# A two-batch double step for the last two hidden slices, closer attention visits, and new places for sums of weights, in a fused attention and SwiGLU kernel

## Chip, core and metric

The kernel runs on one core of a Trainium2 chip. Its metric is the device time of one execution in microseconds. The engines are named as the profile names them: PE is TensorE (matmuls), DVE is VectorE, ACT is ScalarE, POOL is GpSimd, and SP is SyncE, which here only issues DMAs. Each engine works through its own list of instructions in the order of the program, and waits at an instruction until what it needs is there.

## The reference

Sigmoid attention over 8 batches, 12 heads, 448 positions and head width 64, followed by a gated feed-forward block over the 3584 rows that the attention gives:

```python
scores = scale * np.matmul(q, k.transpose(0, 1, 3, 2)) - np.log(S)
attn = 1.0 / (1.0 + np.exp(-scores))
attn_out = np.matmul(attn, v)                 # (8, 12, 448, 64)
x = attn_out.transpose(0, 2, 1, 3).reshape(3584, 768)
g = x @ w_gate                                # (768, 1536)
val = x @ w_val
out = (g * sigmoid(g) * val) @ w_out          # (1536, 768)
```

All inputs and the output are float32.

## The kernel before

**Attention.** The work is cut into 24 units, numbered n = 0 to 23; unit n is four heads of batch n // 3. Its q and k are loaded by SP into four staging slots (`stg_a`, two per unit), cast to 16 bits (`casts`, L843, on POOL from unit 4 on), and transposed by two DMAs on SP's queue (`trans`, L847). Each unit has seven tiles of scores, (n,0) to (n,6): four small matmuls (`qk_tile`, L246), then a sigmoid on ACT (`sig_tile`, L263) into `pt_a`. When all seven are there, 28 small matmuls with v (`pv`, L276) give the rows of x, which DVE copies out of PSUM.

**Feed-forward.** Batches go in pairs, pb = 0 to 3. The hidden width is cut into 12 slices of 128. For pairs 0 and 1 the first half (FFN1) is done slice by slice and batch by batch: `ffn1(b, f)` (L331) has 12 matmuls of 448 columns. Pair 2 did slices 0 to 9, and pair 3 all slices, by *double steps*: `double(pb, (f, f+1))` (L434) takes two slices for both batches of the pair in seven products (a Strassen-Winograd scheme), 7 x 3 x 2 = 42 matmuls, where four `ffn1` units have 48. The scheme needs sums of x (`x_sums`, L411, four kinds for each of three j) and sums of the weights (`fast_w`, L376, kinds 3, 1, 2, 4 for each group of three slices). Kind 4 of x is used in the sixth of the seven products, kind 3 in the fifth.

The second half (FFN2) is always done in the same scheme: `ffn2_group` (L595) is a generator whose seven steps are products of six matmuls of 384 columns, in two PSUM banks in turn; DVE (or ACT) reads each product out before the next but one may write the bank. Groups 0, 1 and 2 take the columns 0 to 383 of each pair's rows, group 3 of pair 1 the rest of pairs 0 and 1. For that rest, `rest_sums` (L584) makes 24 small sums on POOL, in storage that group 0 has used. Sums of the hidden rows are made by `make_sums` (L533) on DVE.

**The order.** A list `units` of FFN work with planned times is merged with the attention *visits* (L955 to L968): a visit makes the score tiles of half a unit, either (n,0) to (n,3) with `pv(n-1)` in its middle, or (n,4) to (n,6). When visit (n,4) to (n,6) has been written into the program, the plan of L951 follows it: POOL waits for the last sigmoid of unit n (`behind_visit`, L864), casts unit n+2, SP transposes it, POOL issues the loads of its v, and SP issues the loads of unit n+4. Below, "visit (n,0)" is the one of four tiles and "visit (n,4)" the one of three.

PSUM is a ring of four tiles of two banks (L72). A group of FFN2 keeps its tile from the first to the last of its seven products (`kept`, L598), and visits go round the rest; when no group is open, a visit of four tiles places its last two so that one of them falls on the fourth tile (L790).

In the second half of pair 1 the products and the visits alternate by the planned list: visit (19,4), four products, visit (20,0), three, (20,4), four, (21,0), three, (21,4), four, (22,0). The other three visits, (22,4), (23,0) and (23,4), stand between the four `ffn1` units of slices 10 and 11. `rest_sums` stands in the first product of `part((1,), ...)` (L753), ahead of visit (19,4). After the last product of group 3 come the sums of x for pair 2, on POOL (L759).

## Time and profile before

| | |
|---|---|
| median of 3 runs | 399.17 us (399.03 to 399.38) |
| the profiled execution, time and span | 399.09 us, 397.1 us |
| PE busy | 386.6 us (97%), 3110 matmuls |
| DVE busy | 251.2 us (63%) |
| ACT busy | 237.4 us (60%) |
| POOL busy | 124.6 us (31%) |
| granted PE clock, mean | 0.999 |
| second half of pair 1 begins | 206.15 us |
| double steps of pair 2 begin, end | 257.32, 297.06 us |

The span runs from the first to the last instruction of the profiled execution; the time of that execution is 2.0 us longer. A line of the timeline gives the start of a run of equal instructions in us from the span's start, its length, engine, line of the kernel, operation, what is written and read, and how many there are; in square brackets stands the time for which the engine had been idle, and who ended it. [...] the pitch of matmuls is read from the starts. The chain of waits is followed back from the last instruction to whatever released it.

### The profile page before, as it was taken

What the parts mean: (1) busy time and instruction counts of PE and PEld (TensorE: products, weight loads), DVE (VectorE), ACT (ScalarE), POOL (GpSimd) and SP (SyncE); (2) the same over time, 40 slices, a digit from 0 to 9 for tenths busy, and PEclk for the clock granted to TensorE, in tenths of its full rate; (3) what the DMA queues carried; (4) which work ended last, traced back from release to release, by engine and by line L of the source; (5) the groups of instructions that cost most, each with busy time, mean ns of one, the idle gap of its engine ahead of it and who ended that gap; (6) DMA issues with size and microseconds to landing.
All of it is one profiled execution on the core that took longest, in us unless ns stands there. A gap on an engine that the chain in (4) does not pass through costs nothing.

```text
span 397.1 us, 8117 instructions
## 1 busy us (share of the span) xinstructions
PE 386.6 (97%) x3110; PEld 201.3 (51%) x3110; DVE 251.2 (63%) x504; ACT 237.4 (60%) x385; POOL 124.6 (31%) x204
## 2 busy tenths in 40 slices
PE   6799999999999999999999999999999999999995
PEld 2444545445555444444455554455556655555663
DVE  2737656688643454466675564799986568787553
ACT  5965885746467787779772567866653066656000
POOL 3638141432311352333337539600007400000900
PEclk9999999999999999999999999999999999999999
DMA  8999989998599777797778699000000520000055
GB/s 254 261 246 256 245 168 215 197 190 118 150 275 241 165 166 161 163 186 164 167 162 199 113 208 238 2 2 1 2 0 2 158 79 2 2 2 0 2 172 146
DMA packets 65590, 54.39 MB, mean 137 GB/s; under 512 B 36048, under 2 KB 61744, under 8 KB 65552
## 3 DMA queue, kind: packets, MB, share of 16 engines
q1 hardware_dynamic: 49264, 36.97, 37.3%
q0 software_dynamic: 15376, 15.34, 24.6%
q10 hardware_dynamic: 912, 1.57, 1.2%
q8 instruction: 24, 0.39, 0.4%
q14 instruction: 14, 0.11, 0.1%
HBM read 47.19 MB, written 11.01 MB: 147 GB/s over the span
## 4 chain that ended last, share of the span: by engine, by line
PE 89%; DMA 4%; DVE 2%; issue 1%; SPq 1%; ACT 1%; POOL 1%; DVEq 0%; POOLq 0%; ACTq 0%
PE ps_D L324 27%; PE ps_D L633 24%; PE ps_D L460 22%; PE ps_D L254 8%; PE ps_D L289 7%; DMA ramp_a<-in_k_dram 2%; DMA stg_a<-in_k_dram 1%; DMA T<-c 1%; PE ps_D L223 1%; POOL c L204 1%; SPq L211 1%; DVE xT L312 0%; DVE T L229 0%; ACT pt_a L273 0%; SPq L166 0%
## 5 line engine op out<-in xcount | busy, mean ns | idle before, releaser
L273 ACT ACTIVATE pt_a<-ps_D 128x896 f16<-128x896 f32 x148 | 127.2, 921 | 40.9 <-PE ps_D L254 39.4
L324 PE MATMUL ps_D<-xT,wg 128*128 128x448 f16 x312 | 69.0, 354 | 0.2
L324 PE MATMUL ps_D<-xT,wv 128*128 128x448 f16 x312 | 68.5, 353 | 0.0
L349 DVE TENSOR_TENSOR t<-ps_D,s 128x448 f16<-128x448 f32 x52 | 32.4, 624 | 54.5 <-ACT s L347 54.0
L470 ACT ACTIVATE snap<-ps_D 128x448 f32<-128x448 f32 x66 | 34.3, 541 | 29.0 <-PE ps_D L460 28.4
L254 PE MATMUL ps_D<-T,T 64*64 64x448 bf16 x644 | 44.1, 357 | 1.6 <-DVE T L229 1.0
L324 PEld LDWEIGHTS <-wg 128*128 128x128 f16 x312 | 27.8, 98 | 33.7 <-issue 11.7
L324 PEld LDWEIGHTS <-wv 128*128 128x128 f16 x312 | 30.4, 98 | 28.6 <-issue 0.4
L347 ACT ACTIVATE s<-ps_D 128x448 f16<-128x448 f32 x52 | 28.7, 552 | 22.6 <-PE ps_D L324 22.6
L633 PEld LDWEIGHTS <-S 128*128 128x128 f16 x312 | 30.2, 98 | 21.1 <-issue 1.4
L633 PE MATMUL ps_D<-ramp_a,S 128*128 128x384 f16 x234 | 40.5, 327 | 0.0
L204 POOL CAST c<-stg_a 128x896 bf16<-128x896 f32 x40 | 36.4, 936 | 12.0 <-DMA stg_a<-in_q_dram 10.7
L289 PE MATMUL ps_D<-pt_a,v 64*64 64x448 f16 x672 | 35.9, 350 | 0.0
L353 DVE SCALAR_TENSOR_TENSOR hT<-ps_D,t 128x448 f16<-128x448 f32 x52 | 32.5, 625 | 5.4
L651 DVE SCALAR_TENSOR_TENSOR osb<-ps_D,osb 128x384 f32<-128x384 f32 x40 | 22.3, 557 | 18.7 <-PE ps_D L633 14.0
L862 POOL CAST held<-S 128x1 bf16<-128x1 f16 x3 | 0.6, 188 | 105.4 <-ACT osb L644 55.7
L646 DVE TENSOR_SCALAR osb<-ps_D 128x384 f32<-128x384 f32 x37 | 20.6, 557 | 19.2 <-PE ps_D L633 16.2
L633 PEld LDWEIGHTS <-hT 128*128 128x128 f16 x228 | 22.1, 98 | 15.6 <-issue 1.2
L460 PE MATMUL ps_D<-xS,wv 128*128 128x448 f16 x132 | 28.6, 353 | 0.0
L862 POOL CAST held<-pt_a 128x1 bf16<-128x1 f16 x13 | 2.5, 189 | 82.0 <-ACT pt_a L273 82.0
L254 PEld LDWEIGHTS <-T 64*64 64x64 bf16 x644 | 15.4, 105 | 24.0 <-issue 16.6
L460 PE MATMUL ps_D<-xT,wg 128*128 128x448 f16 x132 | 26.8, 353 | 0.0
(109 smaller groups left out, 497.7 us busy)
## 6 DMA issues: line engine op xcount, KB each, us to landing
out_dram<-osb SPq DMA_DIRECT2D x45, 192.0 KB, 3.7
stg_a<-in_q_dram SPq DMA_DIRECT2D x18, 448.0 KB, 5.6
stg_a<-in_k_dram SPq DMA_DIRECT2D x18, 448.0 KB, 6.5
v<-in_v_dram POOLq DMA_DIRECT2D x38, 112.0 KB, 4.5
wg<-in_moe_w_gate_dram POOLq DMA_DIRECT2D x4, 576.0 KB, 11.6
wv<-in_moe_w_val_dram POOLq DMA_DIRECT2D x4, 576.0 KB, 12.4
wo<-in_moe_w_out_dram POOLq DMA_DIRECT2D x4, 576.0 KB, 8.4
stg_a<-in_q_dram POOLq DMA_DIRECT2D x3, 448.0 KB, 13.8
```

Source lines behind the costliest of these rows:

```text
L204: eng.tensor_copy(out=t.rearrange("p c h d -> p h c d"), in_=st.rearrange("p h (c d) -> p h c d", c=C))
L254: nc.tensor.matmul(out=sc[g:g + 64, h2, :S], lhsT=kt[r, w * 64:(w + 1) * 64], rhs=qt[r, :, w * 64:(w + 1) * 64], start=True, stop=True,)
L273: nc.scalar.activation(out=pt, in_=sc[:, :, :S], func=SIGM, bias=sbias, scale=qkscale)
L289: nc.tensor.matmul(out=P[g:g + 64, h2, :S], lhsT=vt[r, h2, c * D:(c + 1) * D], rhs=pt[r, h2, :], start=(c == 0), stop=(c == C - 1),)
L324: nc.tensor.matmul(out=D.t[:, i, :S], lhsT=(wg16, wv16)[i][f // FW][:, pr, cs], rhs=xT[(b, pr)], start=(pr == 0), stop=(pr == NP - 1),),
L347: D.read(nc.scalar.activation(out=s16, in_=D.t[:, 0, :S], func=SIGM), 0)
L349: D.read(nc.vector.tensor_tensor(out=t1, in0=D.t[:, 0, :S], in1=s16, op=MULT), 0)
L353: nc.vector.scalar_tensor_tensor(out=hT[(b // 2, f)][:, b % 2, :], in0=D.t[:, 1, :S], scalar=hsc(b // 2), in1=t1, op0=MULT, op1=MULT),
L460: nc.tensor.matmul(out=D.t[:, bank, :S], lhsT=W(f, j), rhs=X(j), start=(start and j == 0), stop=(stop and j == JT - 1), skip_group_check=True,
L470: D.read(nc.scalar.mul(out=o, in_=D.t[:, bank, :S], mul=scale), bank)
L633: nc.tensor.matmul(out=D.t[:, bank, :hw], lhsT=l, rhs=B_(i), start=(first and i == order[0]), stop=(i == order[-1]), skip_group_check=True,),
L651: D.read(nc.vector.scalar_tensor_tensor(out=o, in0=i, scalar=1.0 / hsc(pb), in1=o, op0=MULT, op1=ADD), bank)
```

## The change

Slices 10 and 11 of pair 2 become a sixth double step, so the four `ffn1` units and the visits' places between them go. The second half of pair 1 is cut finer: from visit (19,4) on a visit comes after every two products (the bound on the time between visits falls from 2.0 to 1.5 for units from 19 on). `rest_sums` is called in `part((1,) * 2, ...)`, the part that follows visit (19,4). The sums of x for pair 2 are made on DVE, kinds 1 and 2 among the last products of group 3, kinds 3 and 4 in the first double step; those of pair 3 stay on POOL. The sums of weights for the last three slices are made whole, and once; several sums of weights move to other steps, and they, `rest_h` of pair 3, and the sums of x get other storage. The sums of hidden rows in the double steps of pair 2 are made some steps later (`most`). The `pv` of unit 23 stays ahead of the first double step.

```diff
-    FAST = {LAST - 1: range(0, 10), LAST: range(NF)}
+    FAST = {LAST - 1: range(NF), LAST: range(NF)}
...
+        if (i, kind) == (3, 4):
+            w = FW * 128
+            gT[(i, kind)] = [half_of(ramp_a)[:, 8 * FW * hw + GW:8 * FW * hw + GW + w], pt_f[:, 8 * W2 + GW:8 * W2 + GW + w], half_of(stg_a)[:, 7 * W2:7 * W2 + w]]
+            for j, t in enumerate(gT[(i, kind)]):
+                V.tensor_tensor(out=t, in0=b21[:, j], in1=gT[(i, 2)][:, j], op=SUB)
+            return
...
+    def x_home():
+        t = osp.tile([128, DM], FP32, tag="osb", name=f"xS_{len(xs_free)}_{len(xS)}").bitcast(FP16)
+        xs_free.extend(t[:, i * S:(i + 1) * S] for i in range(3))
...
+    def x_sum(pb, j, n, out):
...
+        a, b, op = {1: (a21, a22, ADD), 2: (old[0], a11, SUB), 3: (a11, a21, SUB), 4: (a12, old[1], SUB)}[n]
+        (G if pb == LAST else V).tensor_tensor(out=out, in0=a, in1=b, op=op)
...
     def rest_h(pb, i):
         if pb == LAST:
-            a, at = pt_f, 5 * JT * FW * 128
+            a, at = [
+                (warm.bitcast(FP16), 0), (half_of(stg_a), 7 * W2 + 384 - 512), (pt_f, 6 * GW - 8 * 128), (pt_f, 8 * W2 + GW + 384 - 10 * 128),
+            ][0 if i < 4 else 1 if i < 8 else 2 if i < 10 else 3]
...
             extra = {
-                (LAST - 1, 0): ((0, 4), (1, 2)), (LAST - 1, 2): ((1, 4), (2, 3)),
-                (LAST - 1, 4): ((2, 1), (2, 2)), (LAST - 1, 6): ((2, 4), (3, 3), (3, 1), (3, 2)),
-                (LAST - 1, 8): ((3, 4),),
-                (LAST, 0): ((4, 3),), (LAST, 2): ((4, 1),), (LAST, 4): ((4, 2),), (LAST, 6): ((4, 4),),
+                (LAST - 1, 0): ((0, 4),), (LAST - 1, 2): ((1, 4), (2, 3), (2, 1)),
+                (LAST - 1, 4): ((2, 2), (2, 4), (3, 3)), (LAST - 1, 6): ((3, 1), (3, 2)), (LAST - 1, 8): ((3, 4),),
             }.get((pb, f), ())
+            if (pb, f) == (LAST - 1, 0):
+                extra = [lambda n=n, j=j: x_sum(LAST - 1, j, n, None) for n in (3, 4) for j in range(NJ)] + extra
+            if (pb, f) == (LAST - 1, 2):
+                units.append((0.0, fast_w, (1, 2)))
...
         elif pb == 1:
             part((0, 1, 0, 1), "1")
             part((0,) * 5)
-            part((1,), "", (lambda: list(rest_sums(1, G)),))
-            part((1,) * 4)
-            part((2,) * 3)
-            part((2,) * 4)
-            part((3,) * 3, "", (skip, lambda: fast_w(1, 3), lambda: fast_w(1, 1)))
-            part((3,) * 4)
-            o_units.append((0.0, sums_of_x, (LAST - 1,)))
+            part((1,))
+            part((1,) * 2, "", (lambda: list(rest_sums(1, G)),))
+            part((1,) * 2)
+            part((2,) * 2)
+            part((2,) * 2)
+            part((2,) * 2, "", (skip, t((0, 3))))
+            part((2,))
+            part((3,), "", (t((0, 1)),))
+            part((3,) * 2, "", (skip, t((1, 3), (1, 1))))
+            part((3,) * 2, "", (t((0, 2)), xs(0)))
+            part((3,) * 2, "", (lambda: [xs(1)(), xs(2)()],))
...
-... since > (3.8 if len(visits[0]) > 3 and visits[0][0][0] < 4 * NJ else 2.0)):
+... since > (3.8 if len(visits[0]) > 3 and visits[0][0][0] < 4 * NJ else 2.0 if visits[0][0][0] < 6 * NJ + 1 else 1.5)):
...
         if fn is double:
-            args[2].append(lambda: make_sums(5))
+            most = args[1][0] - 2 if args[0] == LAST - 1 else 5
+            args[2].append(lambda most=most: make_sums(max(0, most)))
...
-        if fn is ffn1 and args == (2 * LAST - 2, 10):
-            w2 = [lambda a=a: fast_w(*a) for a in ((0, 3), (0, 1), (0, 2))]
-            fill.update({(2 * LAST - 1, 10): w2[:2], (2 * LAST - 1, 11): w2[2:]})
```

## Prediction

> **What bounds the kernel now.** I read the page first: shares of busy time, then the chain.

> ```profile
> PE 386.6 (97%) x3110; PEld 201.3 (51%) x3110; DVE 251.2 (63%) x504; ACT 237.4 (60%) x385; POOL 124.6 (31%) x204
> PE 89%; DMA 4%; DVE 2%; issue 1%; SPq 1%; ACT 1%; POOL 1%; DVEq 0%; POOLq 0%; ACTq 0%
> ```

> PE bounds it. The busy time by stage says whether that holds where the change is (columns: stretch, its length, busy time of PE, PEld, DVE, ACT, POOL, clock, DMA share, GB/s).

> ```profile
> 206.15:242.78 36.63, 36.63 (x341) 20.32 (x337) 20.21 (x39) 18.76 (x28) 19.98 (x42) 1.00 0.93 179
> 242.78:257.32 14.54, 14.54 (x148) 6.91 (x145) 8.73 (x14) 13.05 (x19) 11.36 (x12) 1.00 0.35 86
> 257.32:297.06 39.74, 39.74 (x215) 20.56 (x212) 36.34 (x82) 24.11 (x50) 0.00 (x0) 1.00 0.00 1
> ```

> PE has no idle time from 206 to 297 us, so a matmul taken away is worth its pitch, and any wait put in costs its length. But DMA is busy 0.93 of the first stretch, and visits will follow each other faster there. Hence the timelines of what feeds a visit. PE first:

> ```profile
> 216.00 0.76 PE L254 MATMUL ps_D<-T,T 64*64 64x448 bf16 x12
> 216.70 2.12 PE L633 MATMUL ps_D<-ramp_a,S 128*128 128x384 f16 x12
> ...
> 220.70 0.57 PE L254 MATMUL ps_D<-T,T 64*64 64x448 bf16 x8
> 221.10 1.49 PE L289 MATMUL ps_D<-pt_a,v 64*64 64x448 f16 x28
> 222.43 0.55 PE L254 MATMUL ps_D<-T,T 64*64 64x448 bf16 x8
> 222.91 2.12 PE L633 MATMUL ps_D<-wo,hT 128*128 128x384 f16 x12
> ```

> A visit of three takes 0.70 (216.00 to 216.70), one of four 2.21 (220.70 to 222.91). A product is 0.98, or 1.07 before a visit (219.63 to 220.70), so two with the switch are 2.05. POOL and ACT in the same stretch:

> ```profile
> 211.45 2.34 POOL L593 TENSOR_TENSOR S<-hT,hT 128x128 f16<-128x128 f16 x6 [4.43 <-PE ps_D L633]
> ...
> 218.37 2.34 POOL L593 TENSOR_TENSOR S<-ramp_a,S 128x128 f16<-128x128 f16 x6
> 220.67 0.18 POOL L862 CAST held<-pt_a 128x1 bf16<-128x1 f16 x1
> 220.79 1.80 POOL L204 CAST c<-stg_a 128x896 bf16<-128x896 f32 x2
> 222.54 1.23 POOL L195 DMA_DIRECT2D v<-in_v_dram  x2
> 229.09 0.19 POOL L862 CAST held<-pt_a 128x1 bf16<-128x1 f16 x1 [5.33 <-ACT pt_a L273]
> 229.21 1.81 POOL L204 CAST c<-stg_a 128x896 bf16<-128x896 f32 x2
> ```

> ```profile
> 216.44 2.54 ACT L273 ACTIVATE pt_a<-ps_D 128x896 f16<-128x896 f32 x3 [7.64 <-PE ps_D L254]
> 221.20 0.92 ACT L273 ACTIVATE pt_a<-ps_D 128x896 f16<-128x896 f32 x1 [2.22 <-PE ps_D L254]
> 222.01 0.97 ACT L270 ACTIVATE pt_a<-ps_D 128x448 f16<-128x448 f32 x2
> 222.90 1.73 ACT L273 ACTIVATE pt_a<-ps_D 128x896 f16<-128x896 f32 x2
> ```

> POOL does the 24 sums of L593 from 211.45 to 220.7 (9.26 us, 0.386 each) and only then the casts of unit 21, although the sigmoid that these wait for ended at 218.98. Unit 22's casts start at 229.21 and its visit is at 240.57.

> [...] 189 ns for 448 columns; the trace agrees (six in 1.135 us). [...] the only long rest here, after the last matmul at 392.7, ends with the clock at 0.5 from 396.6. [...] the trace has 1.03 us (L426) for 448 columns against 0.39 (L502).

> **The change part by part.**

> *Slices 10 and 11.* 48 matmuls become 42: 6 x 0.189 = -1.1 us. The visits that stood between them go between products; their number and switches stay.

> *Where POOL's sums stand.* In the built order of the changed kernel the 24 sums come after unit 21's casts and v loads and before unit 22's casts. Step by step: up to visit (19,4) at 216.00 nothing changes; its sigmoids end at 218.98; the casts of 21 follow 0.26 later (229.21 against a sigmoid's end at 228.95), at 219.2. From first cast to the end of v's issue is 2.98 (220.79 to 223.77), so the sums start at 222.2 and end at 231.4, and 22's casts start at 231.55, although the sigmoid they wait for ends near 226.4.

> The transposes follow the casts on SP. The second lands 5.7, 4.5, 7.7 and 4.8 us after its issue (at 206.38, 223.67, 231.67, 241.43); from the first cast that is 7.9, 7.3, 10.2 and 7.1. The 10.2 stood behind four stores and two loads that ended at 235.2; now these are issued 1.5 us sooner and end near 233.7, so I take 7.5: unit 22 can be used at 239.1.

> When does PE want it? From 216.00: three visits of three (2.10), five pairs of products (10.25), two visits of four (4.42) = 16.77, at 232.8. Two waits come on the way. Unit 21 lands at 219.2 + 7.5 = 226.7, and visit (21,0) would be at 226.15: 0.55. And the PSUM ring: with a group open, three tiles are left, so the last tile of a four-visit takes the one whose split sigmoid ends 2.28 after the visit's start (220.70 to 222.98), while PE is there at 1.95 (1.73 plus half of 0.4): 0.4 with the signal. No such case is in the trace, since before these visits stood at a group's end or had a fourth tile; from below it is 0, from above 0.9 if the sigmoids run one late. I take 0.4, twice before (22,0). So PE arrives at 232.8 + 0.55 + 0.8 = 234.1 and waits **5.0** for the transposes.

> After 239.1: the four-visits of 22 and 23, each with 0.4; group 3's first product takes the tile of (22,3), whose sigmoid ends 3.92 after the visit's start (220.70 to 224.62), PE being there at 2.21 + 0.4 + 0.98 = 3.59: another 0.4. Unit 23's casts follow on POOL at 234.7, land by 242 to 245, and are wanted at 246.9: no wait.

> *Sums of x on DVE.* Twelve at 0.39 or 0.32 us; POOL no longer needs 12 x 1.03. Six lie among group 3's last products, where a read of 0.56 is due every 0.98 (218.86, 219.84), and six in the first double step ahead of the read of product five. They write tiles that group 2's and 3's stores empty; group 2's stand behind both transposes of 23 on SP. The last store leaves near 256.5, lands near 259.5 (2.8 to 3.3 us), and the sums end at 260.8; product six wants them at 261.4. Cover 0.6: I take 0, at most 1 if the stores land late.

> *Sums of weights.* In the double steps DVE gets at most three of 0.75 and two of 0.36, or two and four; the fullest step before had 2.9 us of such extras (284.25 to 287.17) and PE did not stop. The first one, in group 2, waits for 23's cast, and the copies of `pv(21)` and two reads are behind it on DVE; it is done at 236.5, during PE's wait. Pair 3 loses four of them and has no idle PE: 0. `rest_h` keeps its twelve copies: 0.

> *Sum.* -1.1 + 0.55 + 5.0 + 4 x 0.4 + 0.4 = +6.4 us. As a walk: 239.1 plus two four-visits with waits 5.22, group 3's wait 0.4, two three-visits 1.40, four pairs 8.20 and `pv(23)` 1.45 is 255.8; six double steps of 7.95 give 303.5 in place of 297.06. Nothing behind it changes. The profiled execution took 399.1 us (its span 397.1): **405.5**; the median of the runs is 0.1 from it.

> **The rivals.**

> *A, as above*: 405.5, own range 404.8 to 406.3 (casts to landing 7.1 to 7.9, ring waits 0 to 0.5 behind the long wait; what is gained ahead of it only lengthens it). Chance 0.50.

> *B, the clock halves in the long wait.* [...] against it, the rest at the end lasted 4.0 before the clock fell. [...] 406.4[...]. Chance 0.28.

> *C, the transposes of 22 wait behind stores* as those of 22 did before (10.2): +2.7, 408.2. For it: DMA share 0.93 here. Chance 0.12.

> *D, POOL is not in the way*: unit 22 lands before 234.1, which needs its casts by 226.6, five us ahead of the chain above; the sums would have to take less than half of their 9.26. Then the ring's waits remain: -1.1 + 0.55 + 2.0, or 400.6. Chance 0.06.

> *E, the other side: the step's gain is what arrives.* The place is visit (22,0), as in D, and the ring's tiles free in time too: 399.1 - 1.1 = 398.0. It decides if 22's casts start by 225.3, when even an unhindered PE (232.8) finds them landed. Against it stands POOL's order. Chance 0.04.

> **The numbers.** The predicted time is A's. B and C reach up, D and E down: 404.4 to 408.2 holds A, and most of B and C, some 8 in 10. A measurement of this kernel tells about 0.2% (0.8 us) from no change. Slower: A to D, 0.96; faster: E, 0.03; the same: 0.01, from D or E half paid.

> **What would show it.** In the changed kernel's trace: PE idle some 5 us ahead of the score matmuls of unit 22, ended by the transposing DMA; L204's pair for unit 22 right behind the 24 small sums, near 231.5; small gaps near 0.4 ended by ACT in the four-visits; six double steps of 7.95, starting near 255.8 and ending near 303.5. I am wrong if the sums run ahead of 21's casts, if the casts land in under 5 us, or if PE's gaps lie in the double steps, where late stores hold DVE's sums of x.

## The result, and the profile after

The changed kernel takes **408.32 us** (median, 407.62 to 409.42) against 399.22 us beside it on the same chip: 1.0231 times as long, interval 1.0206 to 1.0255. The forecast was 405.5 us, range 404.4 to 408.2: the sign and the place are right, the size is 2.8 us short, and the time lies just above the range.

The page of the profiled execution (407.62 us, span 405.8) has the two lines of before again, and one group line that explains them:

```profile
PE 388.2 (96%) x3104; PEld 202.1 (50%) x3104; DVE 254.8 (63%) x516; ACT 240.9 (59%) x391; POOL 112.0 (28%) x192
...
PE 81%; DMA 8%; ACT 2%; POOL 2%; issue 2%; DVE 2%; SPq 2%; DVEq 0%; POOLq 0%; ACTq 0%
...
L254 PE MATMUL ps_D<-T,T 64*64 64x448 bf16 x644 | 45.2, 360 | 7.7 <-DMA T<-c 5.5
```

PE has six matmuls fewer and is nevertheless busy 1.6 us longer; the score matmuls waited 5.5 us for the transposes of Q and K, where the same line of before has 0.2. The busy time by stage (columns: stretch, its length, busy time of PE, PEld, DVE, ACT, POOL, clock, DMA share, GB/s) says where:

```profile
206.15:245.14 38.99, 32.50 (x300) 17.20 (x297) 17.66 (x32) 20.67 (x29) 19.43 (x41) 0.96 0.84 170
245.14:257.65 12.51, 12.26 (x139) 6.24 (x137) 9.46 (x19) 9.66 (x12) 0.00 (x0) 1.00 0.18 44
257.65:305.33 47.68, 47.68 (x257) 24.67 (x253) 44.08 (x99) 29.12 (x60) 0.00 (x0) 1.00 0.06 15
```

The six double steps take 47.68 us with PE always busy, 7.95 each. All of the loss but some 0.4 us lies ahead of 257.65, and in the first stretch the clock was not full either. PE's timeline of that stretch (start, length, and in brackets the idle time before it with its releaser; a length can reach past the next start, as 219.25 + 1.49 = 220.74 does past 220.58, so PE's times are taken from the starts):

```profile
216.10 0.76 PE L254 MATMUL ps_D<-T,T 64*64 64x448 bf16 x12
...
218.85 0.57 PE L254 MATMUL ps_D<-T,T 64*64 64x448 bf16 x8
219.25 1.49 PE L289 MATMUL ps_D<-pt_a,v 64*64 64x448 f16 x28
220.58 0.36 PE L254 MATMUL ps_D<-T,T 64*64 64x448 bf16 x4
221.19 0.38 PE L254 MATMUL ps_D<-T,T 64*64 64x448 bf16 x4 [0.25 <-ACT pt_a L270]
221.50 1.15 PE L627 MATMUL ps_D<-wo,S 128*128 128x384 f16 x6
...
227.43 0.57 PE L254 MATMUL ps_D<-T,T 64*64 64x448 bf16 x8 [1.05 <-DMA T<-c]
...
239.40 0.67 PE L254 MATMUL ps_D<-T,T 64*64 64x448 bf16 x8 [4.45 <-DMA T<-c]
239.85 2.83 PE L289 MATMUL ps_D<-pt_a,v 64*64 64x448 f16 x28
242.46 0.90 PE L254 MATMUL ps_D<-T,T 64*64 64x448 bf16 x8
243.29 1.15 PE L627 MATMUL ps_D<-ramp_a,hT 128*128 128x384 f16 x6
244.93 1.14 PE L627 MATMUL ps_D<-wo,ramp_a 128*128 128x384 f16 x6 [0.49 <-ACT pt_a L273]
```

Four things are to be seen. Visit (20,0) takes 2.65 us (218.85 to 221.50) in place of 2.21, because its last score tile waits for a PSUM tile. Unit 21 is waited for 1.05 us, unit 22 4.45 us. After the long wait `pv(21)` takes 2.83 us in place of 1.49, so it ran at half clock. And the first product of group 3 starts 0.66 us late (243.29 to 244.93 is 1.64, a product 0.98). POOL's timeline shows why unit 22 is late:

```profile
219.33 1.82 POOL L204 CAST c<-stg_a 128x896 bf16<-128x896 f32 x2
...
222.27 2.35 POOL L587 TENSOR_TENSOR S<-hT,hT 128x128 f16<-128x128 f16 x6
...
229.21 2.35 POOL L587 TENSOR_TENSOR S<-ramp_a,S 128x128 f16<-128x128 f16 x6
231.51 0.18 POOL L860 CAST held<-pt_a 128x1 bf16<-128x1 f16 x1
231.63 1.80 POOL L204 CAST c<-stg_a 128x896 bf16<-128x896 f32 x2
```

The 24 sums lie between the casts of unit 21 and those of unit 22, which start at 231.63, although the last sigmoid that their gate waits for had ended at 226.59. The clock around the long wait, in windows of 3.41 us, the length of its stretch at half clock (239.75 to 243.17, within rounding), same columns as above:

```profile
236.34:239.75 3.41, 0.35 (x8) 0.26 (x12) 1.45 (x1) 0.00 (x0) 1.99 (x4) 1.00 1.24 190
239.75:243.17 3.42, 3.42 (x44) 1.51 (x32) 0.37 (x1) 1.80 (x4) 0.00 (x0) 0.50 1.19 212
243.17:246.58 3.41, 2.92 (x28) 1.35 (x24) 1.75 (x4) 1.81 (x3) 0.00 (x0) 1.00 0.22 62
```

The clock fell 0.35 us *after* PE had resumed, and stayed at half for one window in which PE had work all the time. Its changes from here on, at 239.75, 243.17 and 403.59, lie 1 and 47 times 3.41 us apart, so the windows of these tables are laid by them. The other three executions had mean clocks of 0.990, 0.986 and 0.990 and took 408.0 to 409.4; this one had 0.993.

### The profile page after: what moved, and what is told of

It reads as the page before. It is cut to its first block, busy times and chain, and to the rows that moved or that the text cites. A ratio compares the mean times of both kernels' runs of the same rounds, so it can differ in the third digit from the quotient of the medians.

```text
span 405.8 us, 8101 instructions
## 1 busy us (share of the span) xinstructions
PE 388.2 (96%) x3104; PEld 202.1 (50%) x3104; DVE 254.8 (63%) x516; ACT 240.9 (59%) x391; POOL 112.0 (28%) x192
## 3 DMA queue, kind: packets, MB, share of 16 engines
q10 hardware_dynamic: 912, 1.57, 1.2%
## 4 chain that ended last, share of the span: by engine, by line
PE 81%; DMA 8%; ACT 2%; POOL 2%; issue 2%; DVE 2%; SPq 2%; DVEq 0%; POOLq 0%; ACTq 0%
PE ps_D L324 24%; PE ps_D L452 24%; PE ps_D L627 20%; PE ps_D L254 7%; PE ps_D L289 7%; DMA T<-c 4%; ACT pt_a L273 2%; DMA out_dram<-osb 1%; DMA stg_a<-in_k_dram 1%; DMA st<-in_k_dram 1%; POOL c L204 1%; POOL S L587 1%; SPq L211 1%; PE ps_D L223 1%; SPq L557 1%
## 5 line engine op out<-in xcount | busy, mean ns | idle before, releaser
L273 ACT ACTIVATE pt_a<-ps_D 128x896 f16<-128x896 f32 x148 | 127.2, 920 | 42.9 <-PE ps_D L254 42.1
L324 PE MATMUL ps_D<-xT,wg 128*128 128x448 f16 x288 | 63.8, 353 | 0.2
L324 PE MATMUL ps_D<-xT,wv 128*128 128x448 f16 x288 | 63.3, 352 | 0.0
L349 DVE TENSOR_TENSOR t<-ps_D,s 128x448 f16<-128x448 f32 x48 | 29.9, 624 | 49.6 <-ACT s L347 49.1
L462 ACT ACTIVATE snap<-ps_D 128x448 f32<-128x448 f32 x72 | 37.5, 542 | 30.5 <-PE ps_D L452 30.0
L254 PE MATMUL ps_D<-T,T 64*64 64x448 bf16 x644 | 45.2, 360 | 7.7 <-DMA T<-c 5.5
L324 PEld LDWEIGHTS <-wv 128*128 128x128 f16 x288 | 28.1, 98 | 26.4 <-issue 0.4
L324 PEld LDWEIGHTS <-wg 128*128 128x128 f16 x288 | 25.8, 98 | 30.9 <-issue 10.4
L204 POOL CAST c<-stg_a 128x896 bf16<-128x896 f32 x40 | 36.5, 938 | 13.3 <-DMA stg_a<-in_q_dram 8.6
L347 ACT ACTIVATE s<-ps_D 128x448 f16<-128x448 f32 x48 | 26.4, 551 | 22.6 <-PE ps_D L324 22.6
L289 PE MATMUL ps_D<-pt_a,v 64*64 64x448 f16 x672 | 37.3, 359 | 0.2 <-ACT pt_a L273 0.2
L640 DVE TENSOR_SCALAR osb<-ps_D 128x384 f32<-128x384 f32 x37 | 20.6, 557 | 21.2 <-PE ps_D L627 18.0
L353 DVE SCALAR_TENSOR_TENSOR hT<-ps_D,t 128x448 f16<-128x448 f32 x48 | 30.0, 625 | 5.0
L254 PEld LDWEIGHTS <-T 64*64 64x64 bf16 x644 | 15.8, 106 | 31.1 <-issue 17.7
L452 PE MATMUL ps_D<-xS,wv 128*128 128x448 f16 x144 | 31.2, 352 | 0.0
L452 PE MATMUL ps_D<-xT,wg 128*128 128x448 f16 x144 | 29.2, 353 | 0.0
L289 PEld LDWEIGHTS <-v 64*64 64x64 f16 x672 | 20.2, 109 | 13.3 <-issue 1.6
```

The lines of the kernel that those rows point to most:

```text
L204: eng.tensor_copy(out=t.rearrange("p c h d -> p h c d"), in_=st.rearrange("p h (c d) -> p h c d", c=C))
L254: nc.tensor.matmul(out=sc[g:g + 64, h2, :S], lhsT=kt[r, w * 64:(w + 1) * 64], rhs=qt[r, :, w * 64:(w + 1) * 64], start=True, stop=True,)
L273: nc.scalar.activation(out=pt, in_=sc[:, :, :S], func=SIGM, bias=sbias, scale=qkscale)
L289: nc.tensor.matmul(out=P[g:g + 64, h2, :S], lhsT=vt[r, h2, c * D:(c + 1) * D], rhs=pt[r, h2, :], start=(c == 0), stop=(c == C - 1),)
L324: nc.tensor.matmul(out=D.t[:, i, :S], lhsT=(wg16, wv16)[i][f // FW][:, pr, cs], rhs=xT[(b, pr)], start=(pr == 0), stop=(pr == NP - 1),),
L347: D.read(nc.scalar.activation(out=s16, in_=D.t[:, 0, :S], func=SIGM), 0)
```

## The experiments

Two theories stand. **The feeding chain**: visits follow each other faster than POOL's gate, casts, sums and the transposes can feed them; the waits are its, and a halved clock is added by the longest wait. **The rivals**: the clock is not what the excess over the forecast comes from; the transfers of this stretch make the transposes late whatever POOL's order is; or ACT is what PE waits for in the end. The first four kernels ran on one chip (before: 399.48 us there), the last four on another (before: 399.32 us).

**The sums go back where they were**, ahead of visit (19,4); all else is as in the changed kernel.

```diff
-            part((1,))
-            part((1,) * 2, "", (lambda: list(rest_sums(1, G)),))
+            part((1,), "", (lambda: list(rest_sums(1, G)),))
+            part((1,) * 2)
```

> The changed kernel with the 24 small sums back in their old place, ahead of visit (19,4). Theory 1: unit 21's casts slip to 220.9 and its visit waits about 2.1 us, unit 22's casts run at 226.9 and land between 234.3 and 237.1 where PE asks at 235.9, a wait of 0 to 1.2; [...] 402.7 to 404. Rival (the transposes of unit 22 are late because loads and stores stand in front of them, not because of the sums): the long wait stays, 407 to 409.

Measured: 404.25 us (403.87 to 405.33), ratio 1.012, interval 1.0091 to 1.0148. PE's timeline of it at units 21 and 22:

```profile
228.18 0.57 PE L254 MATMUL ps_D<-T,T 64*64 64x448 bf16 x8 [1.48 <-DMA T<-c]
...
237.03 0.57 PE L254 MATMUL ps_D<-T,T 64*64 64x448 bf16 x8 [1.33 <-DMA T<-c]
```

Nearly half of the loss is gone, and with it the long wait; the time is 0.25 us above the range expected. A clock of 1.00 over the whole span of this execution shows that its waits of up to 1.48 us did not halve it. But two waits of 1.4 remain. That of unit 21 has the sums ahead of its casts, which start at 221.19 in place of 219.33. That of unit 22 has none; the chain of waits shows what it has:

```profile
228.89 1.07 SPq L557
...
230.07 1.57 SPq L211
...
231.73 5.25 DMA T<-c
...
237.03 0.41 PE ps_D L254 x4
```

The casts of unit 22 start at 227.15 here. But SP has four stores to issue (L557) before it comes to the transposes (L211), and these land 9.8 us after the first cast, where the changed kernel took 7.7. With 7.7 they would have landed near 234.9 (an estimate), ahead of PE, which was there at 235.70. The place of the sums is thus one part of the cause, not the whole, and the order of SP's queue is another.

**Busy through the wait.** 22 matmuls on zeros stand ahead of visit (22,0), in the PSUM tile that the visit is about to overwrite.

```diff
+        if group[0] == (22, 0):
+            at = ring_at[0]
+            while ring_order[at % 4] in kept:
+                at += 1
+            for i in range(22):
+                nc.tensor.matmul(out=ring[ring_order[at % 4]][:, 0, :S], lhsT=warm[:, :128], rhs=warm[:, :S], start=True, stop=True)
```

> The changed kernel with 22 matmuls of 448 columns on zeros put in front of visit (22,0), so that PE works through most of its long wait (22 x 0.189 = 4.2 of 4.5 us) and nothing else moves. They leave nothing behind: the visit's matmuls overwrite them. Theory 1 (late casts make the wait, and the idle wait halves PE's clock for one or more windows of 3.4 us): the wait's end stays at 239.4, the clock stays full, visit (22,0) takes 2.65 us instead of 3.89, and the time falls to 405.9 (405.5 to 406.4) with runs that agree within 0.4 us. Theory 2 (the excess over my forecast is in the PSUM ring, the transposes or the stores, and the clock is a side effect): 407.6 to 409.4 as the changed kernel.

Measured: 407.59 us (406.77 to 408.8), ratio 1.0197, interval 1.0168 to 1.0225. The range of 405.5 to 406.4 and the spread of 0.4 us that were expected were both missed. Its profiled execution had a full clock at the visit, and from visit (22,0) to the first double step it took 16.69 us (240.49 to 257.18), where the changed kernel took 18.25 (239.40 to 257.65). But it had a half-clock window at the start of the kernel (9.2 to 12.6 us), and visit (19,4) began at 216.94 in place of 216.10. With the changed kernel on another chip the two times were too weak a comparison to decide; it was made again below.

**The sums' late place alone**, put into the kernel before.

```diff
-            part((1,), "", (lambda: list(rest_sums(1, G)),))
-            part((1,) * 4)
+            part((1,))
+            part((1,) * 4, "", (lambda: list(rest_sums(1, G)),))
```

> The kernel before with one edit: the 24 small sums after visit (19,4), as in the changed kernel, at the old distance between visits. Theory 1: unit 22's casts start at 231.5 instead of 229.2 and land near 239.0, before the visit at 240.6: no wait; 399.0 to 399.7. If the place of the sums costs by itself: 404 or more.

Measured: 400.08 us (399.33 to 401.31, 20 runs), ratio 1.0014, interval 1.0005 to 1.0023; the upper end of what was expected is 399.7. The casts of unit 22 start at 231.59 there, as late as in the changed kernel, and its visit still waits only 0.20 us:

```profile
240.92 0.57 PE L254 MATMUL ps_D<-T,T 64*64 64x448 bf16 x8 [0.20 <-DMA T<-c]
```

So late sums cost 0.6 us under the old spacing, and 3.4 to 4.4 under the new one (1.0206 or 1.0231 against 1.012). The new spacing with early sums costs 4.8 us (1.012). Neither the place of the sums nor the spacing of the visits makes the whole loss alone.

**The sums on DVE**, six after each of four parts, so that POOL has none of them.

```diff
+            rs = rest_sums(1, V)
+            six = lambda: [next(rs) for _ in range(6)]
             part((1,))
-            part((1,) * 2, "", (lambda: list(rest_sums(1, G)),))
-            part((1,) * 2)
-            part((2,) * 2)
-            part((2,) * 2)
+            part((1,) * 2, "", (skip, six))
+            part((1,) * 2, "", (skip, six))
+            part((2,) * 2, "", (skip, six))
+            part((2,) * 2, "", (skip, six))
```

> The changed kernel with the 24 small sums on DVE, six at the end of each of four parts, so that POOL has only casts and loads. Theory 1: casts of unit 21 stay at 219.3 (wait 1.05 as before), those of 22 run at 226.8 and land between 234.3 and 237.0 where PE asks at 234.9: wait 0 to 2; the ring's waits of 2.2 us stay; 401.4 to 403.6. If DVE's 24 sums [...] delay its reads of PSUM, up to 1 us more. Rival (DMA queue, not POOL): 407 to 409.

Measured: 405.28 us (403.16 to 406.54), ratio 1.0131, interval 1.0089 to 1.0173. Only the profiled execution, the fastest, lies in the range expected (401.4 to 403.6); what the others lost, the one trace does not show. Its waits for units 21 and 22 are 1.37 and 1.00. That is the result of the sums' old place once more: with POOL free, two waits stay. What is left ahead of the casts is the gate, `behind_visit`, which holds POOL until the last sigmoid of the visit before; the casts of unit 22 start at 227.24. And what is behind them took 9.4 us to the landing of the transposes (236.64), again more than the changed kernel's 7.7.

**The changed kernel and the busy wait again, side by side**, five rounds each; the edit of the second is the one shown above.

> The changed kernel itself, beside the next one on one chip, so that the part of the halved clock can be read from the difference. Theory (long wait of 4.45 us plus a halved clock): 408.3 again, 407.6 to 409.0. If the chip matters more than the kernel: as e2_busy_wait had it here, 407.6.

> The changed kernel with 22 matmuls on zeros ahead of visit (22,0), which keep PE at work while the transposes of unit 22 are on their way. Theory: no halved clock after the wait, so 0.8 to 1.7 us less than e5_after_again, and a smaller spread of its times. Rival (the clock after the wait is not where the excess lies): within 0.4 us of e5_after_again.

Measured: 407.75 us (406.61 to 408.32, ratio 1.0206, 1.0189 to 1.0222) for the changed kernel, 405.97 us (405.72 to 407.15, ratio 1.017, 1.0155 to 1.0186) with the busy wait. The difference of 1.8 us is far above the 0.4 that the rival allowed, and just above the 0.8 to 1.7 of the theory. In the changed kernel's profiled execution the clock fell *during* the wait this time, 2.45 us after the end of PE's last matmul (234.44), and two windows were cold:

```profile
233.48:236.89 3.41, 0.96 (x6) 0.38 (x4) 2.14 (x3) 1.16 (x2) 3.33 (x7) 1.00 0.76 100
236.89:240.30 3.41, 0.69 (x8) 0.37 (x12) 0.43 (x1) 0.00 (x0) 0.93 (x2) 0.50 1.29 201
240.30:243.72 3.42, 3.42 (x40) 1.45 (x32) 0.42 (x1) 1.84 (x4) 0.00 (x0) 0.50 1.19 219
```

PE resumed at 239.61, after a wait of 5.17, and was cold to 243.72: 4.11 us at a clock of 0.50, of which half is lost, 2.05 (an estimate). With the busy wait PE goes from the zeros into the visit at full speed; its timeline:

```profile
234.62 4.33 PE L792 MATMUL ps_D<-warm 128*128 128x448 bf16 x22
239.44 0.57 PE L254 MATMUL ps_D<-T,T 64*64 64x448 bf16 x8 [0.49 <-DMA T<-c]
239.84 1.49 PE L289 MATMUL ps_D<-pt_a,v 64*64 64x448 f16 x28
```

The visit starts at the same time in both (239.61 and 239.44), and the first double step starts at 258.16 and at 256.12: 18.55 us later in one and 16.68 in the other, where the forecast has 16.7 (239.1 to 255.8). Behind the visit, the whole excess over the forecast is thus the clock's; the zeros cost nothing, since PE still waits 0.49 us behind them. The second part of the expectation failed: the spread did not become smaller (1.4 against 1.7 us) although the clocks are 0.998 to 1.0. The landings vary too: unit 21 was waited for 0.40 us in one of these two profiled executions and 1.24 us in the other.

**The gate off.** POOL casts units 21 to 23 as soon as their loads have landed; the sums stay where the change put them.

```diff
-        plan[(n, 4)] = ((behind_visit, n), (ready, n + 2), (load_v, n + 2)) + ((load_qk, n + 4),) * (n + 4 < NQ)
+        plan[(n, 4)] = ((behind_visit, n),) * (n < 6 * NJ + 1) + ((ready, n + 2), (load_v, n + 2)) + ((load_qk, n + 4),) * (n + 4 < NQ)
```

> The changed kernel in which POOL no longer waits for the sigmoids of visits (19,4) to (21,4) before it casts units 21 to 23; the sums stay where they are in POOL's order. Theory (the casts of unit 22 are late because the gate, the casts and the 24 sums stand one behind another): the casts of 21 run near 207, the sums near 209 to 219, the casts of 22 near 219, the transposes land before PE wants them at 232.8, and both long waits go. Left is -1.1 for the matmuls and 1.2 for the waits for PSUM tiles: 399.3. Rival (transfers of this stretch make the transposes late whatever the order): waits on the transposing DMA stay over 2 us, 402 or more.

Measured: 401.1 us (400.14 to 401.46), ratio 1.0043, interval 1.0029 to 1.0057. POOL's timeline of it:

```profile
206.95 1.96 POOL L204 CAST c<-stg_a 128x896 bf16<-128x896 f32 x2
...
211.38 2.34 POOL L587 TENSOR_TENSOR S<-hT,hT 128x128 f16<-128x128 f16 x6 [1.35 <-PE ps_D L627]
...
220.59 1.81 POOL L204 CAST c<-stg_a 128x896 bf16<-128x896 f32 x2
```

The casts of 21 come 12 us sooner, those of 22 11 us sooner. The summary of PE's waits from 200 us on (total, times, longest) no longer has a transpose in it:

```profile
PE ps_D L254 <- ACT pt_a L270: 1.0, 4, 0.2
PE ps_D L627 <- ACT pt_a L273: 0.2, 1, 0.2
```

That decides against the rival as it was put: with the casts sooner, no transpose is waited for. It does not clear the transfers. SP's timeline of it:

```profile
223.11 3.00 SPq L557 DMA_DIRECT2D out_dram<-osb  x4
226.22 6.53 SPq L211 DMA_TRANSPOSE T<-c  x4
```

The casts of unit 22 end at 222.40, but SP issues four stores first. The transposes land at 233.5 for a visit at 233.60: casts 11 us sooner made a landing only 5.9 us sooner, and without the gate it is the order of SP's queue that sets when these transposes start. The expectation of 399.3 was too low, since it counted the waits for PSUM tiles by the brackets of the timeline (1.2 in sum). The visits tell more:

```profile
233.60 0.57 PE L254 MATMUL ps_D<-T,T 64*64 64x448 bf16 x8
...
235.33 0.36 PE L254 MATMUL ps_D<-T,T 64*64 64x448 bf16 x4
235.93 0.38 PE L254 MATMUL ps_D<-T,T 64*64 64x448 bf16 x4 [0.25 <-ACT pt_a L270]
236.25 1.15 PE L627 MATMUL ps_D<-ramp_a,hT 128*128 128x384 f16 x6
237.57 1.14 PE L627 MATMUL ps_D<-wo,ramp_a 128*128 128x384 f16 x6 [0.17 <-ACT pt_a L273]
```

Each visit of four takes 2.65 in place of 2.21, which is 0.44 for a bracket of 0.25, and group 3's first product comes 0.34 late (1.32 against 0.98): 4 x 0.44 + 0.34 = 2.1 us. From visit (19,4) to FFN2 of pair 2 this kernel needs 82.03 us (215.94 to 297.97), the kernel before 81.06 (216.00 to 297.06): +0.97 = 2.1 - 1.1. The gain of the sixth double step is there in full, and the waits for PSUM tiles are larger than it. The median lies 1.0 us above the profiled execution; in what, the one trace does not show.

**Visits in three parts**, on top of the gate's removal: units 20 to 23 are cut 3, 2 and 2, so that no visit wants a fourth score tile while a group is open. The parts of groups 1 to 3 are cut to match, with the same products and sums in them.

```diff
+        if tiles[i][0] > 6 * NJ + 1:
+            visits += [tiles[i:i + 3], tiles[i + 3:i + 5], tiles[i + 5:i + C]]
+            continue
...
-2.0 if visits[0][0][0] < 6 * NJ + 1 else 1.5)
+2.0 if visits[0][0][0] < 6 * NJ + 1 else 0.9 if visits[0][0][0] > 6 * NJ + 1 and visits[0][0][1] else 1.5)
```

> The kernel without the gate, and the visits of units 20 to 23 cut 3, 2 and 2 in place of 4 and 3, with one product between the parts of a unit and two between units; so no visit needs a fourth score tile while a group is open. Theory: the waits for PSUM tiles go, four more switches of 0.09 come: 399.2 - 1.1 + 0.4 = 398.5. Rival (ACT, with 6.6 us of sigmoids in 7.1 us of PE's work per unit, is what PE waits for, however the visits are cut): the waits stay near 1.2 in sum, 399.5 or more.

Measured: 400.67 us (400.34 to 400.86), ratio 1.0032, interval 1.0019 to 1.0045. That is 2.2 us above the expectation, and not to be told from the kernel without the gate, whose interval overlaps. PE's waits from 215 us on:

```profile
PE ps_D L627 <- DVE osb L640: 0.5, 1, 0.5
PE ps_D L452 <- DVE v L488: 0.3, 1, 0.3
PE ps_D L289 <- ACT pt_a L273: 0.2, 1, 0.2
```

The waits for PSUM tiles are gone, so ACT is not the bound that the rival made of it, although the time lies where the rival had it (399.5 or more). From visit (19,4) to the first double step it takes 33.71 us (216.26 to 249.97) in place of 34.35 (215.94 to 250.29): 0.64 less, not 1.7. A part more costs more than the 0.09 that was assumed: the three of unit 20 take 2.02, 0.51 and 0.50 us against 2.21 and 0.70, and the product ahead of a part is longer by 0.1 (1.08 against 0.98), 0.2 in sum. And the plan put no product between units 20 and 21, where two were expected: their score matmuls stand in one row of sixteen, and `pv(20)` waits 0.24 us for ACT behind them. Two waits on DVE then give 0.8 us back. None of these kernels beats the kernel before.

## Why the prediction was right and wrong

*The long wait of unit 22: right.* Casts at 231.55 were forecast and came at 231.63; landing 239.1 came at 239.36; the wait of 5.0 was 4.45, because PE itself arrived at 234.95 in place of 234.1.

*Unit 21: right in kind, 0.55 forecast, 1.05 measured* (0.40 and 1.24 in two other profiled executions). It cost nothing extra in the changed kernel, since it ran into the longer wait.

*The gain of 1.1, the ring's waits of 0.4, the double steps of 7.95, the new homes at nothing: right.* Measured are 1.1 (what closes the sum of the kernel without the gate), 0.44 for each visit of four, 7.95, and no wait in the six double steps. DVE is the exception further on: one product of FFN2 of pair 2 is 0.30 us late on a read of L640, where the prediction had said that nothing behind the double steps changes.

*The clock: wrong, and this is the step that failed.* The prediction's sum has no term for it. It made a rival of it, case B, chance 0.28; its chance and its 406.4 were the author's estimates, with no wait of this length in the trace of before, and the one measured reason, against it, was that the rest at the end lasted 4.0 us before the clock fell. It was halved in both profiled executions of the changed kernel. From visit (22,0) to the first double step they took 18.25 and 18.55 us, against 16.68 with the clock full, so it cost 1.57 and 1.87: close to half of the cold time (1.7 and 2.05, estimates at a clock of 0.50); the bracket of 0.25 that other visits of four have is absent in both. Three things in the traces speak against how the prediction weighed it.

First, work shortly before did not prevent the halving: the 3.41 us ahead of the fall held 0.35 us of PE's work in one case and 0.96 us in the other. Second, PE may work through all of a cold stretch, as from 239.75 to 243.17, where it was busy for 3.42 of 3.42 us. Waits of 4.45 and 5.17 us were followed by 3.4 and 4.1 us of cold work. Third, the rest of 4.0 us at the end was no reason against it: in the repeat the clock fell 2.45 us after PE's last matmul.

With that the profiled execution adds up. Up to FFN2 of pair 2: -1.1 + 1.05 + 4.45 + 3 x 0.44 (visits (20,0), (21,0), (23,0)) + 1.68 for (22,0), which took 3.89 in place of 2.21, + 0.66 for group 3's first product = 8.1, and 8.27 is measured (297.06 to 305.33); the start was 0.1 later. Behind it 0.4 are added, 0.30 of them that read on DVE, which makes the 8.7 us between the spans (397.1 and 405.8). Against the forecast of 405.5 the 2.1 us of this execution are the landing (0.3), the clock (1.6) and the read on DVE (0.3), within rounding. The median lies 0.7 us above this execution, and the other three were longer by up to 1.8 us at lower mean clocks; that they had more cold windows, as in the trace of the repeat, is likely and not shown, since they left no trace. On the second chip the same kernel took 407.75, inside the forecast's range.

*The rivals.* Case D, with POOL out of the way and only the ring's waits left, was put at 400.6 us; the kernel without the gate is this case, at 401.1. But D took the landing to follow the casts by 7.5 us, and there it took 12.9. Case C, 22's transposes behind stores, did not occur in the changed kernel: 7.7 us from cast to landing, where 7.5 was taken. It appears where the sums are out of the way: 9.8 us with the sums early, 9.4 with the sums on DVE. Case E falls by the ring alone: even with nothing late at unit 22, the time is not below that of before.

*What the prediction blamed* was the place of the sums. By the runs the loss has three parts, as ratios to before: 1.0206 as changed, 1.012 with the sums early, 1.0043 without the gate. They come from two chips, so each part is good to some tenths. The sums and the clock that their wait halves are some 3.4 us. The waits that stay with the sums early are some 3.1 us (against a kernel that has the gate off and the sums late); they go with the gate, but the gate is not shown to be their only cause, since the stores ahead of the transposes on SP's queue hold those of unit 22 back as well, and no run has the gate on and these stores moved. The last 1.7 us are the waits for PSUM tiles less the gain of 1.1, of which the trace shows 1.0. The prediction counted only 0.55 for the second part because the long wait hid it.

## What to carry to other kernels

When consumers are moved closer together, compare the new spacing with the whole chain that feeds them before anything else: here visit (19,4) to (21,0) shrank from 14.6 to 10.2 us, while sigmoid, gate, cast and transposes need 11.3 (216.10 to 227.38). A gate that only held a queue back at leisure before becomes part of the bound, and so do the stores in front of the transposes; undoing the most visible delay leaves both in place. And a forecast wait on PE as long as those measured here should be priced with cold work behind it: 1.57 and 1.87 us came on top of waits of 4.45 and 5.17, while waits of up to 1.48 left the clock at 1.00.

## What was not expected of the hardware

```profile
400.18:403.59 3.41, 1.06 (x7) 0.41 (x5) 1.12 (x2) 0.00 (x0) 0.00 (x0) 1.00 0.61 149
403.59:405.80 2.21, 0.00 (x0) 0.00 (x0) 0.00 (x0) 0.00 (x0) 0.00 (x0) 0.50 0.13 41
...
393.13:396.54 3.41, 1.49 (x10) 0.69 (x7) 1.25 (x3) 0.00 (x0) 0.00 (x0) 1.00 0.49 119
396.54:399.10 2.56, 0.00 (x0) 0.00 (x0) 0.00 (x0) 0.00 (x0) 0.00 (x0) 1.00 0.27 76
```

A window with 1.06 us of work was followed by half the clock, one with 1.49 us was not. In three of the profiled executions, those of the busy wait's first run, of the sums on DVE and of the repeat of the changed kernel (mean clocks 0.996, 0.996 and 0.985), a half-clock window also stood at the start of the kernel (8.2 to 11.6 us in the repeat), with full clock before and after it; in the first trace of the changed kernel there was none. There PE's busy time does not tell the cases apart: from 5.0 to 8.2 us it was 1.77 us in the repeat, whose clock then fell, and 1.37 us in the first trace, whose clock stayed at 1.00.

A bracket of 0.25 us in a visit stands for 0.44 us of PE's time: the idle time that a timeline names is only a part of what a stop costs, and the distance between the starts of the instructions around it is the measure.
